# An mLSTM layer with a top-1 mixture of experts on one core: first token lists gathered a step sooner without their gates, gates fetched by a second gathering, and an opening with other fills, copies and an earlier embedding

## The chip, the core and the metric

One core of one Trainium2 chip runs the kernel. Its engines work side by side and wait for each other by semaphores: TensorE (PE in the rows; PEld is its loading of weights), VectorE (DVE), ScalarE (ACT), GpSimd (POOL) and SyncE (SP), which here only issues transfers. The metric is device time in microseconds (us) of one execution; lower is better. In the rows of the profile POOL's and SP's queues are marked POOLq and SPq.

## The reference

The first half is a recurrent layer with gates (4 batches, 8 heads, 768 time steps, 40 dimensions per head), the second a mixture of 8 experts in which each of the 3072 tokens goes to the one expert with the largest logit.

```python
for t in range(S):                                   # q, k, v: (4, 8, 768, 40)
    m_new = np.maximum(f_gate[:, :, t] + m, i_gate[:, :, t])
    f_stab = np.exp(f_gate[:, :, t] + m - m_new)
    i_stab = np.exp(i_gate[:, :, t] - m_new)
    m = m_new
    C = f_stab * C + i_stab * einsum('bhd,bhe->bhde', vt, kt)
    n = f_stab * n + i_stab * kt
    y[:, :, t] = sigmoid(o_gate[:, :, t]) * (C @ qt) / np.maximum(np.abs(n . qt), 1.0)
x = y.transpose(0, 2, 1, 3).reshape(3072, 320)

xn, en = x / (norm(x) + 1e-6), emb / (norm(emb) + 1e-6)
logits = xn @ en.T / tau
expert_idx = argmax(logits, axis=1)
gate_w = softmax(logits)[arange(N), expert_idx]
for e in range(8):                                   # w1: (8, 320, 1024), w2: (8, 1024, 320)
    mask = expert_idx == e
    out[mask] = gate_w[mask, None] * (np.maximum(x[mask] @ w1[e], 0.0) @ w2[e])
```

## The kernel before

The recurrence is worked in 24 steps (NS; `for n in range(NS)`, line 1213), each of them 128 time steps of one batch with its 8 heads; tile n is block n // 4 of batch n % 4. In each step TensorE forms the scores of the next tile (`stage_scores`), the products of k with u·v that update the state (`stage_add`), the output y (`stage_y`) from the weighed scores and the state, the transposes of an earlier x (`stage_xt`) and the logits of a still earlier one (`stage_logits`). VectorE weighs the scores (`stage_weigh`), scales the state (`stage_next`), divides y (`stage_den`, `stage_x`); GpSimd forms u·v (`stage_uv`) and multiplies x by its output gate (`stage_gate`; VectorE in the last two steps); ScalarE copies the state for y (`stage_mid`, `stage_keep`), applies the sigmoids and sums squares. `stage_store` writes x to `x_d` in DRAM, whose rows have 336 columns: 320 of x and 16 that all hold the token's gate weight.

The order is written out by hand: every engine has one queue and works it in the order of the program text. The opening (lines 1012 to 1086) loads the first tiles, keeps TensorE at work with products that nobody reads (`fill`, FILLS), and computes the first block's gate factors. The later blocks' factors come from a chain: `gates_ends`, `gates_chain` (a scan over the blocks, between two groups of three copies across partitions by `same`, all on VectorE, ahead of the loop), `gates_floor` and `gates_exp` in steps 0 and 1, `gates_turn` in step 2. ScalarE's exponential and sigmoid need different tables; small instructions on `maxc` (lines 1076, 1236, 1291) load them ahead of use. The expert embeddings are scaled in steps 2 to 4 (`embeddings`, EMB_AT) and are first used by the logits of step 4.

Tokens are routed in three groups of tiles, 0 to 5, 6 to 12, 13 to 23 (GROUPS). The table ROUTE (line 954) says in which step which part runs: the products of a step are issued at once, its VectorE work goes into a queue `vq`, of which `tick(9)` takes nine instructions a step and the next `route` the rest. After the second group `early_ids` writes `ids_a`: for each of the two fullest experts the first 256 of its tokens among tiles 0 to 12. `gates_early` has three parts for the gate weights of these 13 tiles: [0] root, [1] share, both on VectorE, and [2], the DMA that puts the weights into columns 320 to 335 of `x_d` (line 472). Step 20 issues [2], step 21 the gathers (`gather_a`, four indirect DMAs by GpSimd's queue into `xs_a`, 128 rows each). Step 23 transposes `xs_a` on TensorE (`x_tile`, line 352), and after the loop the hidden products of these two experts (`first_hidden`, `mm1`, line 374) fill TensorE while the third group is routed. Their outputs are scaled by the gates in `xs_a` (`first_out`, `mm2_out`) much later, under the hidden products of the two experts' second halves, whose rows come by `gather(slots_b)` (line 1445). The weights of an expert are loaded raw by SP and split into a high and a low part (`piece`, lines 195 to 198), those of the first expert in the steps of W1_AT.

The places that the change touches in the loop:

```python
            if n == NS - 4:
                gates_early[2]()
            ...
                    stage_gate(k, G if n < NS - 2 else V)
            ...
            if n == NS - 3:
                for i in range(NE * HT):
                    gather_a(*divmod(i, HT))
```

## Time and profile before

| what | value |
| --- | --- |
| median of 3 runs | 322.53 us (321.46 to 325.38) |
| the profiled execution | 318.54 us |
| its span, first to last instruction | 316.8 us |
| mean granted clock of TensorE | 0.985 of full speed |
| busy: TensorE, its weight loads, VectorE, ScalarE, GpSimd | 93%, 89%, 68%, 53%, 53% |
| DMA traffic | 63.32 MB, mean 200 GB/s |

The rows further down are of that one profiled execution, with times from the start of its span. A busy TensorE is not one at its peak: its matmuls are pipelined and their ends modelled. A wait is put down to what came last. The share of an engine over the whole span is a mean over stages: the opening, the steps of the recurrence, the end of the routing, and the experts.

### The profile page before, as it was taken

What the parts mean: (1) busy time and instruction counts of PE and PEld (TensorE: products, weight loads), DVE (VectorE), ACT (ScalarE), POOL (GpSimd) and SP (SyncE); (2) the same over time, 40 slices, a digit from 0 to 9 for tenths busy, and PEclk for the clock granted to TensorE, in tenths of its full rate; (3) what the DMA queues carried; (4) which work ended last, traced back from release to release, by engine and by line L of the source; (5) the groups of instructions that cost most, each with busy time, mean ns of one, the idle gap of its engine ahead of it and who ended that gap; (6) DMA issues with size and microseconds to landing.
All of it is one profiled execution on the core that took longest, in us unless ns stands there. A gap on an engine that the chain in (4) does not pass through costs nothing. (4 is left out here: it accounts for less than half of the span.)

```text
span 316.8 us, 9586 instructions
## 1 busy us (share of the span) xinstructions
PE 296.0 (93%) x3637; PEld 281.9 (89%) x3637; DVE 216.4 (68%) x608; ACT 167.1 (53%) x429; POOL 168.7 (53%) x205
## 2 busy tenths in 40 slices
PE   7798999999994999999999899999999999999992
PEld 3788989999883899899999689999999999999991
DVE  5776798979983479856744986575576685787520
ACT  7575866776872485343343564355457267255310
POOL 7877867778786288140765622620830822633112
PEclk9999999999999699999999999999999999999998
DMA  6898887989899641130588949959639949646001
GB/s 203 303 297 302 254 266 223 311 258 272 282 252 270 215 138 41 13 88 2 180 260 228 310 161 212 326 156 344 152 117 266 259 137 320 165 119 206 23 24 38
DMA packets 47962, 63.32 MB, mean 200 GB/s; under 512 B 21018, under 2 KB 37862, under 8 KB 47906
## 3 DMA queue, kind: packets, MB, share of 16 engines
q1 hardware_dynamic: 45234, 54.16, 57.3%
q0 software_dynamic: 2560, 8.35, 8.6%
q8 instruction: 31, 0.51, 0.7%
q14 instruction: 25, 0.20, 0.2%
q10 hardware_dynamic: 112, 0.10, 0.1%
HBM read 47.51 MB, written 11.93 MB: 188 GB/s over the span
## 5 line engine op out<-in xcount | busy, mean ns | idle before, releaser
L425 POOL DMA_INDIRECT out<-ob,ids x20 | 22.4, 1121 | 77.0 <-DVE ob L422 66.9
L376 ACT ACTIVATE hh<-ph 128x448 fp32r<-128x448 f32 (+2 forms) x48 | 23.4, 490 | 39.9 <-PE ph L374 29.1
L406 PE MATMUL po<-w2h,hl 128*128 128x320 f32 x128 | 39.6, 309 | 0.0
L406 PE MATMUL po<-w2h,hh 128*128 128x320 f32 x128 | 39.6, 309 | 0.0
L406 PE MATMUL po<-w2l,hh 128*128 128x320 f32 x128 | 39.5, 309 | 0.0
L556 POOL TENSOR_TENSOR uv<-kv_s,u_t 64x328 f32<-64x328 f32 x47 | 35.1, 747 | 6.7 <-PE c L610 4.0
L374 PE MATMUL ph<-xh,w1h 128*128 128x448 f32 (+2 forms) x96 | 32.1, 337 | 2.0 <-DVE hh L381 2.0
L379 DVE SCALAR_TENSOR_TENSOR hl<-ph,hh 128x384 fp32r<-128x384 f32 (+1 forms) x48 | 24.4, 508 | 11.5 <-ACT hh L376 11.4
L374 PE MATMUL ph<-xh,w1l 128*128 128x448 f32 (+2 forms) x96 | 32.0, 336 | 0.0
L195 ACT CAST w1h<-raw 128x512 fp32r<-128x512 f32 x48 | 29.0, 612 | 5.3 <-POOL halves L1468 2.9
L571 PE MATMUL s<-kq_s 128*64 128x64 f32 x768 | 28.3, 226 | 2.6 <-DVE w_s L580 2.1
L571 PEld LDWEIGHTS s<-kq_s 128*64 128x64 f32 x768 | 26.1, 141 | 3.9 <-DVE w_s L580 2.8
L198 DVE TENSOR_TENSOR w2l<-raw,w2h 128x320 fp32r<-128x320 f32 x58 | 27.6, 523 | 1.2 <-issue 0.4
L195 ACT CAST w2h<-raw 128x320 fp32r<-128x320 f32 x62 | 24.9, 458 | 6.3 <-DMA raw<-in_w 6.1
L422 DVE TENSOR_SCALAR ob<-po,gt 128x320 f32<-128x320 f32 x16 | 8.8, 550 | 27.4 <-PE po L406 27.4
L198 DVE TENSOR_TENSOR w1l<-raw,w1h 128x512 fp32r<-128x512 f32 x36 | 25.5, 717 | 1.5 <-ACT w1h L195 1.4
L297 POOL DMA_INDIRECT xs<-x_d,ids x20 | 22.1, 1103 | 6.2 <-issue 5.8
L374 PE MATMUL ph<-xl,w1h 128*128 128x448 f32 (+2 forms) x96 | 24.5, 336 | 0.0
L653 PE MATMUL y<-uv,w_s 128*64 128x82 f32 x384 | 24.2, 245 | 0.0
L406 PEld LDWEIGHTS po<-w2h,hh 128*128 128x128 f32 x128 | 24.0, 188 | 0.0
L406 PEld LDWEIGHTS po<-w2l,hh 128*128 128x128 f32 x128 | 24.0, 188 | 0.0
L406 PEld LDWEIGHTS po<-w2h,hl 128*128 128x128 f32 x128 | 24.0, 188 | 0.0
(315 smaller groups left out, 891.7 us busy)
## 6 DMA issues: line engine op xcount, KB each, us to landing
raw<-in_w SPq DMA_DIRECT2D x32, 320.0 KB
kv_s<-in_kv SPq DMA_DIRECT2D x24, 324.0 KB
kq_s<-in_kq SPq DMA_DIRECT2D x48, 160.0 KB
raw<-in_w SPq DMA_DIRECT2D x14, 512.0 KB
raw<-in_w SPq DMA_DIRECT2D x18, 256.0 KB
sig<-in_og SPq DMA_DIRECT2D x24, 160.0 KB
x_d<-x SPq DMA_DIRECT2D x24, 160.0 KB
x_d<-halves SPq DMA_DIRECT2D x4, 576.0 KB
```

The lines of the kernel that those rows point to most:

```text
L195: A.copy(h, src)
L198: (eng or V).tensor_tensor(lo, src, h.bitcast(F32), ALU.subtract)
L297: G.indirect_dma_start(out=xs[0 : c.shape[0], a], out_offset=None, in_=x_d[0:rows], in_offset=bass.IndirectOffsetOnAxis(ap=c, axis=0), bou ...
L374: T.matmul(ph, lt, rh, start=i == 0, stop=i == len(ops) - 1)
L376: A.activation(hh, ph, AF.Relu)
L379: V.scalar_tensor_tensor(hl[:, 0:m], ph[:, 0:m], 0.0, hh[:, 0:m].bitcast(F32), ALU.max, ALU.subtract)
L406: T.matmul(po[0 : ts_.stop - ts_.start, 0:DM], lt[f][:, ts_], rh[:, f], start=k == 0, stop=k == len(ops) - 1)
L422: V.tensor_scalar(ob, po[0:r, 0:DM], gate, None, ALU.mult)
L425: store = G.indirect_dma_start(out=out, out_offset=bass.IndirectOffsetOnAxis(ap=slots, axis=0), in_=ob, in_offset=None, bounds_check=NT - ...
L556: eng.tensor_tensor(uv[n % NB][rows, :, :, r], list(rows_of(n))[1][rows], u_t[rows, j, b].unsqueeze(3).broadcast_to([L, 2, NP, D1]), ALU.mult,
L571: T.matmul(s[r * L : r * L + L, c, p], k_of(n, odd)[:, a, cs], q_of(n)[:, a, cs], start=True, stop=True,)
L653: T.matmul(yh[c][:, g, :, odd], w_s[n % NB][:, c, 2 * g + odd], uv[n % NB][:, c, 2 * g + odd], start=g + odd == 0, stop=n < B and c == 0, ...
```

## The change

The fills become 11, 1 and 1, and the second and third place, which called none before, call them: behind the first gate products and behind the clearing of the sums. The copies across partitions of the gate chain go to ScalarE; the gathering copies stand behind `stage_mid` of step 0, the scan and the copies back behind the weighing of the second scores. `gates_floor` computes what `gates_exp` needs first, with a tile `low` of its own. The embeddings' last part stands before `stage_next` of step 4, and that step's logits behind `stage_add`. The x tiles are two named tiles of 336 columns whose last 16 are cleared once; the first 13 stores write all 336. The list `ids_a` is computed in step 19, root and share of the early gates in steps 20 and 21, their store behind the last x store. The gathers are issued in step 20 and once more behind `gather(slots_b)`. VectorE takes the gating from step 20 on, and u·v of the last tile, in step 21. One weight piece moves from step 19 to 18.

```diff
@@ -48,7 +48,7 @@
-W1_AT = (11, 13, 15, 17, 19, 21)
+W1_AT = (11, 13, 15, 17, 18, 21)
 W_AT = (9, 10, 12, 14, 16, 18, 19, 20, 21, 22, 22, 23)
@@ -58,7 +58,7 @@
 ROOTS = {6: (0, 4), 10: (4, 8), 15: (8, 13), 18: (13, 16), 22: (16, 20)}
-FILLS = (9, 3, 3)
+FILLS = (11, 1, 1)
 NK = 2
@@ -521,7 +521,8 @@
-        st, sigs, xs_, grp = {}, {}, {}, {}
+        st, sigs, grp = {}, {}, {}
+        xs_ = [tp.tile([P, B, XW], F32, name=f"x_{i}", bufs=1) for i in range(2)]
@@ -686,12 +687,9 @@
         def x_of(n):
-            return xs_[n // B][:, n % B].rearrange("p (h d) -> p h d", h=H)
+            return xs_[n // B % 2][:, n % B, 0:DM].rearrange("p (h d) -> p h d", h=H)
         def stage_x(n):
-            j, b = divmod(n, B)
-            if b == 0:
-                xs_[j] = tp.tile([P, B, DM], F32, name=f"x_{j}", tag="x", bufs=2)
             den = st[n]["den"].rearrange("p a r -> p (a r)")
@@ -701,17 +699,18 @@
             j, b = divmod(n, B)
-            SY.dma_start(xrows(j)[:, b, 0:DM], xs_[j][:, b])
+            w = XW if n < GROUPS[1][1] else DM
+            SY.dma_start(xrows(j)[:, b, 0:w], xs_[j % 2][:, b, 0:w])
...
             junk = tp.tile([P, DM], F32, name=f"junk_{n}", tag="junk", bufs=1)
-            A.activation(junk, xs_[j][:, b], AF.Square, accum_out=ss_all[:, j, b : b + 1])
+            A.activation(junk, xs_[j % 2][:, b, 0:DM], AF.Square, accum_out=ss_all[:, j, b : b + 1])
...
             j, b = divmod(n, B)
-            x = xs_[j][:, b]
+            x = xs_[j % 2][:, b]
             px = pX.tile([P, 512], F32, name=f"px_{n}", tag="px")
@@ -962,11 +961,12 @@
             15: ([], [(route_a, 1)]),
-            16: ([lambda: route_rank(1)], [(route_b, 1), (route_sum, 1), (gates_early[0],)]),
+            16: ([lambda: route_rank(1)], [(route_b, 1), (route_sum, 1)]),
             17: ([], [(route_os, 1)]),
             18: ([early_count], [(route_c, 1), (early_base,)]),
-            19: ([lambda: route_ids(1)], [(gates_early[1],), (route_d, 1)]),
-            20: ([], [(early_ids,)]),
+            19: ([lambda: route_ids(1)], [(route_d, 1), (early_ids,)]),
+            20: ([], [(gates_early[0],)]),
+            21: ([], [(gates_early[1],)]),
         }
@@ -1071,11 +1071,13 @@
                 )
+        fill(FILLS[1])
         V.tensor_copy(u_t[:, 0].rearrange("p b c a -> p c b a"), pg[:, 0:NH].rearrange("p (c b a) -> p c b a", c=2, b=B))
...
         clear_sums()
+        fill(FILLS[2])
         stage_scores(0)
@@ -1088,39 +1090,37 @@
         mm = ap1.tile([NH, NW + 1], F32, name="mm")
-        mj, aj, na, cl, gam = (ap1.tile([NG, NK], F32, name=nm) for nm in ("mj", "aj", "na", "cl", "gam"))
+        mj, aj, na, cl, gam, low = (ap1.tile([NG, NK], F32, name=nm) for nm in ("mj", "aj", "na", "cl", "gam", "low"))
         flag = ap1.tile([NG, NK], BF16, name="flag")
...
-        def same(dst, src):
-
-            V.tensor_tensor(dst, src, src, ALU.max)
-
         def gates_ends():
-            same(fp[:, :, 0], gs[:, :, P - 1])
+            V.memset(mm[:, 0:1], -1e30)
+            V.tensor_tensor(fp[:, :, 0], gs[:, :, P - 1], gs[:, :, P - 1], ALU.max)
             V.tensor_tensor(fp[:, :, 1], gp[:, :, P - 1], gs[:, :, P - 1], ALU.add)
+        def gates_gather():
+            for jj in range(NJ):
+                A.copy(fpj[:, :, :, jj], fp[jj * NH : (jj + 1) * NH].rearrange("p k w -> p w k"))
+
         def gates_chain():
-            for jj in range(NJ):
-                same(fpj[:, :, :, jj], fp[jj * NH : (jj + 1) * NH].rearrange("p k w -> p w k"))
-            V.memset(mm[:, 0:1], -1e30)
             f, p = (fpj[:, w].rearrange("p k j -> p (k j)") for w in range(2))
...
             for jj in range(NJ):
-                same(mj[jj * NH : (jj + 1) * NH], mm[:, jj : jj + NJ * (NK - 1) + 1 : NJ])
+                A.copy(mj[jj * NH : (jj + 1) * NH], mm[:, jj : jj + NJ * (NK - 1) + 1 : NJ])
...
             V.tensor_tensor(gam, mj, aj, ALU.subtract)
+            V.tensor_scalar(low, gam, -RANGE, None, ALU.max)
+            for k in range(NK):
+                V.scalar_tensor_tensor(
+                    gp[:, k], gp[:, k], na[:, k : k + 1], low[:, k : k + 1].broadcast_to([NG, P]), ALU.add, ALU.max
+                )
             V.tensor_tensor(cl, mj, gi[:, :, 0], ALU.max)
...
             V.tensor_scalar(flag, cl, -RANGE, None, ALU.is_lt)
-            V.tensor_scalar(cl, gam, -RANGE, None, ALU.max)
-            for k in range(NK):
-                V.scalar_tensor_tensor(
-                    gp[:, k], gp[:, k], na[:, k : k + 1], cl[:, k : k + 1].broadcast_to([NG, P]), ALU.add, ALU.max
-                )
@@ -1209,7 +1209,6 @@
         gates_ends()
-        gates_chain()
         for n in range(NS):
@@ -1229,6 +1228,8 @@
             stage_mid(n)
+            if n == 0:
+                gates_gather()
             for k in of(n - 1, 1, NEXT_AT):
@@ -1238,28 +1239,32 @@
                 stage_scores(n + 1)
-            if n + 2 < NS and n not in (1, 2):
+            if n + 2 < NS - 1 and n not in (1, 2):
                 stage_uv(n + 2)
             if n == 0:
-                for t in (ent, *c_st):
+                for t in (*(x[:, :, DM:] for x in xs_), ent, *c_st):
                     G.memset(t, 0.0)
-            if n == NS - 4:
-                gates_early[2]()
             if n:
...
                 for k in of(n, 1):
-                    stage_gate(k, G if n < NS - 2 else V)
+                    stage_gate(k, G if n < NS - 4 else V)
             if n == 1:
                 stage_uv(n + 2)
-            if n == NS - 3:
+            if n == NS - 4:
                 for i in range(NE * HT):
...
                 stage_weigh(n + 1)
+            if n == 0:
+                gates_chain()
+            if n == EMB_AT[2]:
+                embeddings(2)
             for k in of(n, 1, NEXT_AT):
                 stage_next(k)
+            if n == NS - 3:
+                stage_uv(n + 2, (V, V))
             if n != EMB_AT[2]:
@@ -1272,10 +1277,6 @@
                 stage_uv(n + 2)
-            if n == EMB_AT[2]:
-                embeddings(2)
-                for k in of(n, 3, (EMB_AT[2],)):
-                    stage_logits(k)
             if last:
@@ -1285,6 +1286,9 @@
                 stage_add(n, 1)
+            if n == EMB_AT[2]:
+                for k in of(n, 3, (EMB_AT[2],)):
+                    stage_logits(k)
             if n != 1:
@@ -1370,6 +1374,7 @@
         stage_store(n)
+        gates_early[2]()
         work(1, 2)
@@ -1443,6 +1448,8 @@
     xs = gather(slots_b)
+    for i in range(NE * HT):
+        gather_a(*divmod(i, HT))
     halves = lp.tile([P, NTT, 2, 3 * P], U16, name="halves", bufs=1)
```

## Rows read from the trace of the kernel before

**Rows 1.** The page: busy us, share of the span and instructions of each engine.

```profile
PE 296.0 (93%) x3637; PEld 281.9 (89%) x3637; DVE 216.4 (68%) x608; ACT 167.1 (53%) x429; POOL 168.7 (53%) x205
```

**Rows 2.** Waits of PE, whole span: who for whom, us in total, times, longest.

```profile
PE pa L352 <- DMA xs_a<-x_d,ids_a: 5.2, 1, 5.2
...
PE s L571 <- DVE w_s L580: 2.1, 3, 1.4
...
PE pm L730 <- DVE ent L1201: 1.1, 1, 1.1
```

**Rows 3.** Stretches: busy us (x instructions) of each engine, granted clock, DMA share, GB/s.

```profile
88.00:98.30 10.30, 9.84 (x255) 9.01 (x251) 7.77 (x27) 7.03 (x23) 7.19 (x9) 1.00 0.92 237
98.30:103.40 5.10, 0.00 (x0) 0.00 (x1) 1.02 (x3) 0.31 (x2) 4.17 (x5) 0.90 0.98 306
103.40:109.20 5.80, 5.77 (x47) 5.29 (x48) 2.46 (x8) 2.67 (x8) 1.31 (x3) 0.50 0.79 256
109.20:130.00 20.80, 20.48 (x200) 19.70 (x200) 17.71 (x43) 12.57 (x36) 14.20 (x13) 1.00 0.25 72
139.50:150.00 10.50, 10.24 (x79) 9.98 (x78) 4.70 (x17) 2.93 (x7) 0.00 (x0) 1.00 0.06 18
```

**Rows 4.** Timeline at the list and its gathers: start, us, engine, line, operation.

```profile
90.77 0.16 DVE L937 TENSOR_TENSOR pad_a<-thrp,cnt_a 128x4 f32<-128x4 f32 x1
...
91.17 0.72 DVE L947 TENSOR_SCALAR ids_a<-pad_a 128x4 uint32<-128x4 f32 x1
...
91.96 0.40 SPq L472 DMA_DIRECT2D x_d<-sw  x1
...
97.11 1.31 POOL L297 DMA_INDIRECT xs_a<-x_d,ids_a  x1 [2.80 <-DMA x_d<-sw]
```

**Rows 5.** The tile xs_a: its gathers (ns min/median/max), and issue to landing.

```profile
L297 POOL DMA_INDIRECT xs_a<-x_d,ids_a x4: 994/1000/1306, 97.1 to 101.3; - x4
DMA to landing us min/median/max: 5.4/6.0/6.2
```

**Rows 6.** Timeline, DVE: prices of root, share, gating and a u·v half.

```profile
6.50 0.49 DVE L556 TENSOR_TENSOR uv<-kv_s,u_t 64x328 f32<-64x328 f32 x1
...
77.95 0.45 DVE L451 TENSOR_TENSOR lg_all<-lg_all,rs 128x104 f32<-128x104 f32 x1
...
85.78 0.79 DVE L458 RECIPROCAL sn<-sn 128x104 f32<-128x104 f32 x1
...
88.53 0.37 DVE L468 COPY sw<-se 128x208 f32<-128x208 f32 x1
...
95.68 0.49 DVE L700 TENSOR_TENSOR x<-x,sig 128x320 f32<-128x320 f32 x1
...
122.54 1.03 DVE L451 TENSOR_TENSOR lg_all<-lg_all,rs 128x88 f32<-128x88 f32 x1
```

**Rows 7.** Timeline of the opening.

```profile
1.10 4.02 PE L996 MATMUL warm<-ones 128*128 128x512 bf16 x9 [1.10 <-DVE ones L510]
...
7.43 1.98 PE L571 MATMUL s<-kq_s 128*64 128x64 f32 x32
...
10.27 1.15 PE L571 MATMUL s<-kq_s 128*64 128x64 f32 x32 [0.32 <-DVE w_s L580]
...
11.16 1.28 ACT L1291 ACT_TABLE_LOAD   x1
...
11.57 1.01 DVE L1097 TENSOR_TENSOR fpj<-fp 32x4 f32<-32x4 f32 x3
...
13.77 0.69 DVE L580 TENSOR_TENSOR w_s<-s,late 128x512 f32<-128x512 f32 x1
...
15.50 0.46 PE L653 MATMUL y<-uv,w_s 128*64 128x82 f32 x8
```

**Rows 8.** Timeline, POOL behind the second lists' gathers.

```profile
150.08 1.02 POOL L425 DMA_INDIRECT out<-ob_a,ids_a  x1 [10.65 <-DVE ob_a L424]
```

**Rows 9.** Timeline, PE at step 4.

```profile
28.09 0.87 PE L730 MATMUL pm<-ent,xt 128*64 128x8 f32 x24 [1.12 <-DVE ent L1201]
```

## The prediction

> **What bounds the kernel now.** I read the busy shares first: TensorE (PE) is busy 93% of the span and no other engine comes near [rows 1], so what can be won is time in which PE waits or runs slowly. PE's waits come next: one of 5.2 us for the first gathered lists, 2.1 us in three for the weighed scores, 1.1 us for the scaled embeddings [rows 2]. The table by stretches shows what the long wait costs beyond itself [rows 3]: from 98.3 to 103.4 PE does nothing, and from 103.4 to 109.2 its granted clock is 0.50, the lower of its two levels (1.2 instead of 2.4 GHz), while PE is busy all the time. Half of those 5.8 us is lost, 2.9. So the place costs 5.1 + 2.9 = 8.0 us. From 109.2 to 130 PE is busy 20.48 of 20.8 us: what PE gains before it moves the end.
>
> Why are the lists late? `ids_a` is computed from 90.77 to 91.17 + 0.72 = 91.9. SyncE issues the store of the gates at 91.96, and GpSimd (POOL) holds the first gather until 97.11, the last 2.8 us of it for that store alone [rows 4]. The four gathers start from 97.1 to 101.3, 1.4 apart, and each takes 5.4 to 6.2 us from issue to landing [rows 5]. The first lands at 97.1 + 6.2 = 103.3, where PE starts again.
>
> **Part 1, lists and gathers.** The list moves from step 20 of the state loop to 19, the gathers from 21 to 20, the gates' store behind the last x store. On VectorE (DVE) the gates' root moves from 16 to 20 and their share from 19 to 21. In before the share runs from 85.78 to 88.53 + 0.37 = 88.9, ahead of the addition that the list needs [rows 6]. Without it that addition starts near 85.9, and the list, 1.1 us as in before, is there at 87.2. POOL comes later: in before it was free for the gathers at 97.11 − 2.80 = 94.3, in step 21. From the second weighing at 13.77 [rows 7] to the end of the last step's logits at 98.3 are 23 steps, 3.7 us each, so one step earlier is 90.6; one gating fewer on POOL brings it forward, the weight piece that moves from step 19 to 18 does not delay it further than that. Between 90 and 91, then: the first lands at 96.0 to 97.2, the second at 97.4 to 98.6. PE asks for them at 98.3 and about half a us later. The wait goes, with 1 to 2 us in hand for the first, and with it the fall of the clock: 8.0 gained.
>
> What is late next? DVE. Into steps 20 to 22 come two gatings at 0.49, two u·v halves at 0.49, the share at 3.1 us (an estimate of 2.2 if nothing slows its long instructions), and the root, whose large instruction took 0.45 in one place and 1.03 in another [rows 6]; with its two small ones I estimate 0.8 to 2.0. The list's 1.1 leaves. Sum: 0.98 + 0.98 + (2.2 to 3.1) + (0.8 to 2.0) − 1.1 = 3.9 to 6.0. DVE was busy 7.77 of the 10.3 us from 88.0 to 98.3, and 0.9 of that was the share's tail, which is in the sum already [rows 3]. So 3.0 to 5.1 us come into 2.5 us of slack: 0.5 to 2.6 shows at PE, and 5.1 if the order in DVE's queue lets none of the slack be used. But the next step's weighing stands ahead of root and share in the queue, so PE meets each delay a step later, by which time part is made good. I take 1.5. Part 1 gives 6.5; its ends are 8.0 − 5.1 = 2.9 and 8.0.
>
> The rest of part 1 is costed at nothing, by its cover. The x stores of 13 tiles become 5% wider (336 columns for 320); two small clearings stand on POOL behind the u·v of step 2. The second gathering is four more indirect DMAs, behind the second lists' own: POOL stands idle for 10.65 us up to 150.08 [rows 8], from 139.4; 4 x 1.4 = 5.6 us fit in. The first of them lands at 139.4 + 6.2 = 145.6 or earlier (DMA is at 0.06 there [rows 3]), the last at 149.8; the first row of gates is wanted just before the store at 150.08, the others later. Without that cover each us of late gates would hold DVE's queue and, behind it, the evictions of PE's hidden products.
>
> **Part 2, the opening.** The nine filling products take 4.02 us, 0.43 each, which for 512 columns is 1.2 GHz. The first scores (32 products) take 1.98, the second scores 1.15 [rows 7]. So the clock rises between 9.4 and 10.3. Behind the nine fills PE has short pauses. Eleven fills reach to about 1.10 + 11 x 0.43 = 5.8 and hold the first gate product by some 0.25; the two single ones fill pauses. If unbroken work lifts the clock before the first scores, these take 1.98 − 1.15 = 0.8 less and their additions about 0.3 less; less the 0.25, 0.9 gained. If not, the fills cost 0.25 to 0.6.
> By the Trainium skill (TensorE: Matmul & The Clock Gate, "What's actually happening") the half rate is the default, activity releases it, and the monitor runs freely, not from the kernel's start; by it the sum holds the 0.9 in some executions and not in others.
>
> The chain of gate maxima moves too. In before DVE copies across partitions, three in 1.01 us and three back, ahead of the weighing of the second scores: ready at 10.27 + 1.15 = 11.4, weighed at 13.77. Now ScalarE (ACT) makes these six copies, as an estimate 0.15 each, and the weighing comes first, near 11.6. But ACT has its own chain: a sigmoid, a table load of 1.28 [rows 7], then the copy of the mid state that the second y reads. That load ran at 11.16, under DVE's chain; now it stands behind the gates: 11.5 + 0.5 for the gather, 0.2 for the scan, 0.5 for the copies back, 0.5 for the sigmoid, 1.3 + 0.2 for the load, 0.6 for the mid state, 15.3. The second y began at 15.50 [rows 7]. So here almost nothing is gained, and some 0.4 at the next scores, whose weighing has fewer floors ahead of it. Opening in all: 1.3 at best, −0.6 at worst; taken 0.8, nearer the good end because in before too the clock rose once PE worked without pauses.
>
> **Part 3, the embeddings.** PE waits 1.12 us at step 4 for `ent` [rows 9], which DVE copies behind two scalings of the state. Now it copies first, and the logits stand behind y and the additions. The wait goes whole; taken 1.0 (0.5 if y then meets the later scalings). The stretches from step 5 on show no such wait to swallow it [rows 2].
>
> **Sum.** 6.5 + 0.8 + 1.0 = 8.3, taken as 8. The profiled execution took 318.54 us, 316.8 of span and 1.74 around it: 310.5. It lies 4.0 below the median of the runs shown, 322.53; no row says what those lost, so I take the same 8 from the median: 314.5.
>
> **Rivals.** (a) VectorE takes the gathers' place: no slack is used, steps 20 to 23 grow by 5.1, part 1 leaves 2.9; with 1.8 elsewhere 4.7, so 317.8. For it: DVE is busy 0.75 of that stretch before anything is added [rows 3]. Against it: the queue order above. (b) The gathers still land late: their 6 us belong to a stretch with DMA at 0.92 to 0.98 [rows 3]; at 9 us, or with POOL held a step longer, a wait of 3 us stays and the clock falls with it. Then some 1.5 of part 1 and 1.8 elsewhere remain: 319.2. Against it: the four landings lie within 0.8 us of each other [rows 5].
> The Trainium skill (SBUF — State Buffer, "SBUF: two separate sides") says that DVE copies in a two-port mode keep GpSimd from writing descriptors, so that gathers beside DVE work starve. Here the longest generation is 1.31 us against a median of 1.00 [rows 5], which bounds it; by the rule a landing moves by the length of such copies, 0.37 for the share's last.
> (c) Slower: VectorE's 5.1 comes as one gap of PE in steps 21 to 23 and the clock falls there. 9 us of work at half rate lose 4.5; 5.1 + 4.5 − 8.0 = 1.6, and with fills that cost 0.6 and embeddings at 0.5 the sum is 1.7 slower: 324.2. It decides if PE stands still there in one piece, as it did from 98.3 until its clock fell. (d) Everything hits: 8.0 + 1.3 + 1.1 = 10.4, so 312.1.
>
> **How the numbers follow.** Forecast 0.62, with its own range 312.5 to 317 (6.5 ± 1.2 of part 1 and the two ends of the opening), (a) 0.15, (b) 0.10, (c) 0.06, (d) 0.07. The range 309.5 to 319.5 holds the forecast, (d) with 2.6 to spare for what the runs' 4 us hide, (a) and most of (b); it leaves out (c) and tails, under 2 in 10. Two per cent, about what a measurement of this kernel can tell from no change, is 6.45 us, so faster needs 316.1 or less: (d) and nine tenths of the forecast, 0.62. Slower means 329: the far end of (c) and what I did not think of, 0.06. The rest is 0.32.
>
> **What would show it.** Right: no wait of PE for `xs_a`; granted clock 1.00 from step 20 through the tail; the first gather issued near 90 us; first scores near 1.2 us; no wait for `ent`. Wrong: PE waiting for `w_s` or x in steps 21 to 23 by over 2 us; a clock of 0.50 in the 90s; DVE waiting for `xs_a` at the first outputs with PE held behind; hidden products of the first lists waiting for weights that still land at the old time.

## The result, and the profile after

The changed kernel takes 325.54 us (median of 20 runs, 322.85 to 329.30) where the kernel before takes 322.36 (20 runs, 319.42 to 328.01). The ratio is 1.0124, with a 95% interval of 1.0097 to 1.0152: slower by 1.2%. Ratios here leave out executions that took over 1.5% longer than the quickest of the same kernel, so they need not be the quotient of the two medians. The forecast was 314.5, the range 309.5 to 319.5. The direction was wrong, and rival (c), the slower one, is not what happened either.

The waits of TensorE in the changed kernel (columns: engine, instruction, what it waited for, total us, times, longest):

```profile
PE pt L338 <- DVE xl_p L341: 3.1, 1, 3.1
PE ph L374 <- issue: 2.5, 1, 2.5
PE s L572 <- issue: 1.9, 2, 1.0
PE s L572 <- DMA kq_s<-in_kq: 1.5, 2, 1.0
PE y L665 <- ACT c_mid L627: 1.2, 1, 1.2
PE c L611 <- DVE c L634: 1.2, 1, 1.2
```

The waits for `xs_a` and for `ent` of [rows 2] are both gone, as predicted. In their place stand waits of which [rows 2] shows next to nothing. "issue" means that PE waited for nothing that the profile shows. In the steps of the recurrence up to 88 us its own next instructions were not there (last section); the 2.5 us, ahead of 162.53, are another thing: PE follows VectorE's `hl_b`, and that ScalarE's `hh_b`, held until 161.64 as told below. The stretches that answer to [rows 3], with 40 to 60, the stretch behind PE's longest wait and one near the end added (columns: us, then busy us and instructions of each engine, granted clock, DMA share, GB/s):

```profile
40.00:60.00 20.00, 18.06 (x459) 16.48 (x454) 15.44 (x55) 12.15 (x39) 12.71 (x16) 1.00 0.90 288
98.30:103.40 5.10, 4.74 (x80) 4.43 (x78) 4.76 (x13) 2.46 (x8) 2.28 (x3) 0.67 0.41 150
103.40:109.20 5.80, 5.75 (x108) 5.23 (x105) 5.20 (x16) 4.52 (x15) 0.10 (x1) 1.00 0.60 176
140.00:150.00 10.00, 6.93 (x41) 6.65 (x40) 2.32 (x7) 1.65 (x3) 2.93 (x3) 0.84 0.22 63
146.80:150.10 3.30, 3.30 (x14) 3.30 (x13) 1.03 (x5) 0.58 (x1) 0.00 (x0) 0.50 0.00 0
160.00:200.00 40.00, 37.03 (x227) 35.81 (x227) 26.50 (x64) 18.24 (x39) 20.38 (x21) 0.96 0.80 227
```

From 103.4 to 109.2 PE now does 108 instructions at the full clock, where it did 47 at half. But from 140 to 150 it does 41 where there were 76 from 140 to 150 before, and it is idle for 3.1 us. Behind the gaps the granted clock falls: it is 0.50 from 99.0 to 102.3 and again from 146.8 to 150.1, a sign of being wrong that the prediction named ("a clock of 0.50 in the 90s"). The timelines of PE, ScalarE and POOL show what stands there (start, duration, instruction, and in brackets the idle time before it with what ended it):

```profile
140.64 0.60 PE L338 MATMUL pt<-ident,xs 128*128 128x128 f32 x4
...
138.18 0.38 ACT L376 ACTIVATE hh_a<-ph 128x256 fp32r<-128x256 f32 x1 [0.43 <-remote]
144.86 1.07 ACT L340 CAST xh_p<-pt 128x512 fp32r<-128x512 f32 x2 [6.29 <-remote]
...
138.63 0.99 POOL L297 DMA_INDIRECT xs_a<-x_d,ids_a  x1 [0.30 <-issue]
142.54 1.00 POOL L297 DMA_INDIRECT xs_a<-x_d,ids_a  x1 [0.30 <-issue]
```

The cast of the later slots' rows waits only for PE's transposes. The records of the first four of them end by 141.24. It begins at 144.86, 1.3 us after POOL has issued the last gather of the second gathering. "remote" means that the page finds no instruction that ended just before the release. The trace has the times at which semaphores rise, and they tell more: the cast waits for a semaphore that only TensorE's instructions raise, and the rises for these four products stand at 144.73 to 144.84, 3.6 us or more behind the ends of their records. So it is TensorE's signal that comes late here, not ScalarE that is slow. VectorE's rest `xl_p` and the third turning wait behind it. The same thing stands in steps 21 and 22, where the first gathering now runs (POOL issues it from 92.95 to 98.3): two engines stand still until about the time that POOL is done, and TensorE's signals of 94.59 and 95.37 rise at 98.12 and 98.95.

```profile
98.15 0.69 DVE L581 TENSOR_TENSOR w_s<-s,late 128x512 f32<-128x512 f32 x1 [3.31 <-remote]
98.98 0.48 ACT L719 COPY xt<-px 128x384 f32<-128x384 f32 x1 [3.14 <-remote]
```

The table follows the lead through the kernel: starts of some weighings `w_s`, of the first hidden products, and the span, each from the trace named. The first two columns are the traces of [rows 1] and of the result; the next two are from one chip ("chip 0"), the last from another ("chip 6"). Both are experiments below.

| us | before | changed | before, chip 0 | changed, chip 0 | changed, chip 6 |
| --- | --- | --- | --- | --- | --- |
| weighing of step 6 | 32.27 | 30.68 | 32.78 | 29.97 | 30.38 |
| step 10 | 48.13 | 45.93 | 48.09 | 45.45 | 45.81 |
| step 12 | 54.85 | 55.05 | 55.16 | 55.23 | 54.10 |
| step 18 | 77.12 | 78.09 | 77.43 | 78.54 | 76.12 |
| step 21 | 89.94 | 90.35 | 90.25 | 91.74 | 88.49 |
| first hidden product of the first lists | 107.90 | 107.56 | 105.91 | 108.23 | 101.52 |
| first hidden product of the later slots | 145.94 | 150.14 | 143.95 | 150.60 | 139.00 |
| span | 316.8 | 323.3 | 317.5 | 323.7 | 310.4 |

The lead of 2.2 us at step 10 is lost by step 12; the sooner lists leave 0.3 us at the first hidden product; at the later slots' product the changed kernel is 4.2 behind, at the end 6.5. The medians differ by less than these spans, 3.2 us: both traces of before are of executions below its median (318.5 and 319.3 us, where its runs beside these kernels lay between 317.6 and 328.0). Nor is the lead always lost by step 12: `e1` below, the same program up to there, weighs steps 12 and 18 at 53.02 and 75.07.

### The profile page after: what moved, and what is told of

The parts are those of the page before. It is cut to its first block, busy times and chain, and to the rows that moved or that the text cites. A ratio compares the mean times of both kernels' runs of the same rounds, so it can differ in the third digit from the quotient of the medians.

```text
span 323.3 us, 9613 instructions
## 1 busy us (share of the span) xinstructions
PE 300.6 (93%) x3641; PEld 284.5 (88%) x3641; DVE 218.3 (68%) x606; ACT 168.1 (52%) x435; POOL 171.1 (53%) x207
## 4 chain that ended last, share of the span: by engine, by line
PE 73%; DVE 12%; another core or an unknown queue 5%; DMA 3%; ACT 2%; issue 2%; POOL 0%; POOLq 0%; SPq 0%; DVEq 0%
PE ph L374 28%; PE po L406 17%; PE s L572 5%; PE po_b L406 4%; PE y L654 4%; DMA kq_s<-in_kq 3%; PE c L611 3%; PE po L391 3%; PE y L665 3%; DVE op L895 2%; PE pm L729 2%; PE px L715 1%; PE po_a L406 1%; DVE w_s L581 1%
## 5 line engine op out<-in xcount | busy, mean ns | idle before, releaser
L557 POOL TENSOR_TENSOR uv<-kv_s,u_t 64x328 f32<-64x328 f32 x45 | 33.8, 750 | 7.1 <-PE c L611 2.9
L572 PE MATMUL s<-kq_s 128*64 128x64 f32 x768 | 29.2, 227 | 3.4 <-issue 1.9
L572 PEld LDWEIGHTS s<-kq_s 128*64 128x64 f32 x768 | 26.9, 141 | 4.4 <-issue 3.2
L198 DVE TENSOR_TENSOR w1l<-raw,w1h 128x512 fp32r<-128x512 f32 x36 | 27.3, 769 | 0.0
L198 DVE TENSOR_TENSOR w2l<-raw,w2h 128x320 fp32r<-128x320 f32 x58 | 26.5, 503 | 0.6
L581 DVE TENSOR_TENSOR w_s<-s,late 128x512 f32<-128x512 f32 x24 | 16.5, 687 | 12.4 <-PE s L572 9.0
```

Of the source, the lines that this page charges most:

```text
L198: (eng or V).tensor_tensor(lo, src, h.bitcast(F32), ALU.subtract)
L557: eng.tensor_tensor(uv[n % NB][rows, :, :, r], list(rows_of(n))[1][rows], u_t[rows, j, b].unsqueeze(3).broadcast_to([L, 2, NP, D1]), ALU.mult,
L572: T.matmul(s[r * L : r * L + L, c, p], k_of(n, odd)[:, a, cs], q_of(n)[:, a, cs], start=True, stop=True,)
L581: V.tensor_tensor(w_s[n % NB].rearrange("p c a t -> p (c a) t"), st[n]["s"].rearrange("p c a t -> p (c a) t"), late.unsqueeze(1).broadcast ...
```

## Experiments

Ratios are to the kernel before, run beside each kernel on the same chip.

**One part taken away or alone (chip 11; before 319.03).** `e1_no_second` leaves the second gathering out, and with it the gates of these lists:

```diff
     xs = gather(slots_b)
-    for i in range(NE * HT):
-        gather_a(*divmod(i, HT))
```

> The changed kernel without its second gathering: the four lists keep the rows' gates at zero, so their part of the output is left out; everything else stays. Theory S: ScalarE's cast of the rows xh_p, which in the changed kernel begins 3.6 us after its transposes (144.86, with the extra gathers on POOL from 138.63 to 143.54), is held by the second gathering. Then the cast follows the transposes within 0.2 us as before, and the time falls by 4 to 5 us below the changed kernel's 325.5, to about 321. Theory R: the stall has another cause (instructions that arrive late, whatever the gathers do) and the loss sits in the recurrence, where the scores of step 21 came 2 us later. Then the time stays at 325 within 1 us, and a stall of some us stands in the same place or near it.

Measured: 313.77 us, 0.9914 (0.9872 to 0.9955). `e2_second_early` keeps the second gathering and moves it:

```diff
         work(3)
         tick(9)
+        for i in range(NE * HT):
+            gather_a(*divmod(i, HT))
         route_rank(g)
```

> The changed kernel with the second gathering moved ahead: POOL issues it right after the rows' last turning in the drain (about 110 us) instead of behind the gathering of the later slots (138.6). Theory S (the gathers hold ScalarE's cast because they are under way when it is due): about 321, no stall at the cast; POOL's splits of weights behind them come 5.2 us later and have 6.6 us of POOL's idle time before the later slots' gathering to hide in. Theory R: 325 within 1 us. If the gathers hold whatever ScalarE does at the time: a stall of 3 to 6 us on ScalarE at 113 to 120 us in place of the other, and 325 again.

Measured: 312.22 us, 0.9853 (0.9782 to 0.9925). `e3_opening` is the kernel before with FILLS = (11, 1, 1), the two new fills, the copies on ScalarE and the chain behind the weighing:

> The kernel before with the opening's part alone (more filling products in other places, the gates' copies on ScalarE, the chain behind the weighing). Prediction on record: 0.4 to 0.8 us gained. Rival: the second step's y waited 1.20 us for the copy c_mid of ScalarE in the changed kernel, and the scores of the second step for their input (1.05 and 0.41 us), so the opening gives nothing: within 0.5 us of the kernel before, 322.4.

Measured: 318.07 us, 0.9997 (0.9936 to 1.0059). The clock was up at the first scores (1.15 us for the 32 products, against 1.98 in [rows 7]), but the second scores then waited 0.83 us for `kq_s`. No gain can be seen. With the old fills the first scores take 1.98 us in two traces of four (the one of [rows 7] and e17) and 1.15 in the other two (e4, e6), so the faster clock is not always a gain of the new fills. `e4_lists` is the kernel before with the lists' part alone:

> The kernel before with the lists' part alone: the first lists gathered sooner without gates, the gates in a second gathering, VectorE's and POOL's work moved; the opening and the embeddings stay as before. Prediction on record for this part: 6.5 us gained, 316. Theory S: the gain of the sooner lists (about 1 to 2 us by the changed kernel's trace, where the first hidden product stands 0.9 us sooner) less 5 us at the cast: about 326. Theory R, where the loss is in the recurrence and comes from the opening or the embeddings: about 321.

Measured: 315.44 us, 0.9948 (0.9901 to 0.9994), near neither theory's number. e1 and e2 lie 7 and 9 us under the 321 of theory S: none of these four traces shows a "remote" stall on ScalarE or VectorE, so on this chip there was nothing for either theory to explain. What they show is the wait that the prediction expected next, VectorE's queue. In e1, VectorE (lines between them left out):

```profile
92.83 0.68 DVE L581 TENSOR_TENSOR w_s<-s,late 128x512 f32<-128x512 f32 x1
93.43 1.01 DVE L557 TENSOR_TENSOR uv<-kv_s,u_t 64x328 f32<-64x328 f32 x2
94.48 0.80 DVE L458 RECIPROCAL sn<-sn 128x104 f32<-128x104 f32 x1
...
97.48 0.37 DVE L468 COPY sw<-se 128x208 f32<-128x208 f32 x1
97.77 0.16 DVE L683 SCALAR_TENSOR_TENSOR den<-y,e_t 128x8 f32<-128x8 f32 x1
...
99.40 0.69 DVE L581 TENSOR_TENSOR w_s<-s,late 128x512 f32<-128x512 f32 x1
```

and PE:

```profile
100.14 0.55 PE L352 MATMUL pa<-ident,xs_a 128*128 128x128 f32 x3 [1.81 <-DVE w_s L581]
```

The u·v halves and the share, from 93.43 to 97.85, stand ahead of the denominators and so of the last weighing; PE's turning of the gathered rows needs the scores' PSUM tile, which that weighing frees. This wait stands in seven traces of this study, 1.8 to 1.9 us long.

**The changed kernel, the kernel before and two variants (chip 0; before 322.23).** `e5_after_again` and `e6_before_again` are the two kernels unchanged, `e2b_second_early` is e2 again, and `e7_share_22` is e2 with one edit more:

```diff
-            21: ([], [(gates_early[1],)]),
+            22: ([], [(gates_early[1],)]),
```

> The changed kernel once more, unchanged, beside its variants on one chip. The moved second gathering stood at 0.985 of the kernel before, the kernel without it at 0.991. If the second gathering in its old place costs 4 to 5 us whenever it runs: 1.005 to 1.012 of the kernel before, with ScalarE's cast xh_p 3 us or more behind its transposes. If the stalls of 3 to 6 us on ScalarE and VectorE (98, 145 and 162 us) belong to that one execution and not to the program: 0.985 to 0.995 of the kernel before, and no such stall in this trace.

> The kernel before, unchanged, to see its trace a second time. The prediction took its 5.15 us wait for the first lists' rows as the cost of every execution. If it is: PE waits 4.5 to 5.5 us before the rows' turning. If the wait is only what is left when PE runs ahead (the opening alone showed 0.77 us there, with the last product of the recurrence 2.1 us later): the wait is 1 to 5 us, and the later the recurrence's end, the shorter. Ratio 1.000 within 0.6%.

> The changed kernel with the second gathering ahead in the drain, once more, beside the changed kernel on the same chip. If the place of the second gathering decides: 0.980 to 0.990 of the kernel before and 1.5 to 2.5% under the changed kernel. If it does not: within 0.5% of the changed kernel.

> The same with one edit more: the shares of the gates (VectorE, 3.2 us: six operations from the reciprocal to the copy sw) run at step 22 in place of 21. In the runs so far they stand ahead of the step's denominators, and so ahead of the last weighing w_s, on VectorE, and PE waits 1.8 us for w_s before it turns the first rows. If VectorE's queue is what holds the end of the recurrence: that wait is gone and the time 1 to 2 us under the kernel with the second gathering moved alone. If it only moves the wait (the turned rows' rests xl_a stand behind the shares then): within 0.5 us of it.

Measured: e5 324.50 us, 1.0112 (1.0060 to 1.0164); e6 322.71, 1.0000; e2b 321.86, 1.0009 (0.9957 to 1.0062); e7 322.28, 0.9999 (0.9954 to 1.0044). The stall at the cast is in e5 again:

```profile
145.37 1.07 ACT L340 CAST xh_p<-pt 128x512 fp32r<-128x512 f32 x2 [6.22 <-remote]
```

Moving the second gathering into the drain takes it away and is worth 1.0% (1.0112 to 1.0009), some 3 us. In e2b the cast follows its transposes:

```profile
142.33 0.59 ACT L340 CAST xh_p<-pt 128x512 fp32r<-128x512 f32 x1 [2.88 <-PE pt L338]
```

POOL issues the second gathering there from 122.0 to 127.0, and no engine has unexplained idle time; between 122.9 and 126.4 no signal of TensorE is due. The kernel before shows no 5 us wait here, but VectorE, ScalarE and PE held while POOL issues the first gathering (95.9 to 101.1). From e6, VectorE, ScalarE and two of PE's five small gaps:

```profile
101.88 0.17 DVE L682 SCALAR_TENSOR_TENSOR den<-y,e_t 128x8 f32<-128x8 f32 x1 [3.93 <-remote]
...
101.98 0.60 ACT L626 COPY c_mid<-c 40x164 f32<-40x164 f32 x2 [3.27 <-remote]
...
100.31 0.34 PE L730 MATMUL pm<-ent_p,xt 128*64 128x8 f32 x5 [0.39 <-issue]
101.03 0.34 PE L730 MATMUL pm<-ent_p,xt 128*64 128x8 f32 x5 [0.39 <-issue]
```

e7 settles nothing: here the held `w_s` (3.28 us at 99.84) covers the queue that it was to shorten.

**What of a gather holds the engines (chip 13; before 319.54).** `e8_twice` runs the loop of the second gathering twice (`range(2 * NE * HT)`); `e9_narrow` reads as many rows, 64 bytes each, from a view of `x_d` with 16 columns:

```diff
-        gather_a(*divmod(i, HT))
+            out=xs_a[:, e, a, 0:16],
+            in_=x_d.rearrange("r (g o) -> (r g) o", o=16)[0 : GROUPS[1][1] * P],
```

> The changed kernel with its second gathering done twice: eight gathers of 128 rows behind those of the later slots, where it has four (the output stays the same). In its two traces ScalarE's cast xh_p began 1.3 us after POOL had issued the last gather (143.5 and 144.9), though its transposes had ended 3 us earlier. Theory H (ScalarE gets its next instruction only when POOL has issued its gathers): four gathers at 1.30 us each more, the cast comes 5.2 us later still, and the time is 4 to 5 us above the changed kernel, about 1.025 of the kernel before. Theory F (one piece of ScalarE's program arrives late, once): the cast stays 3.5 us behind its transposes, the time within 1 us of the changed kernel.

> The changed kernel with a second gathering of as many rows but 64 bytes of each in place of 1344 (the rows' gates stay zero, so the four lists' part of the output is left out). If the bytes of the gathered rows hold ScalarE's cast: it follows its transposes within 1 us, and the time is 3 to 4 us below the changed kernel, about 1.000 of the kernel before. If it is POOL's issuing of descriptors, whatever they move: the same stall of 3 us or more, within 1 us of the changed kernel.

Measured: e8 329.11 us, 1.0281 (1.0128 to 1.0433); e9 325.18, 1.0202 (1.0111 to 1.0293). The cast, in e8 and in e9:

```profile
147.53 0.58 ACT L340 CAST xh_p<-pt 128x512 fp32r<-128x512 f32 x1 [9.10 <-remote]
```

```profile
143.46 1.07 ACT L340 CAST xh_p<-pt 128x512 fp32r<-128x512 f32 x2 [6.30 <-remote]
...
141.15 1.00 POOL L1453 DMA_INDIRECT xs_a<-x_d,ids_a  x1 [0.30 <-issue]
```

With a twentieth of the bytes the stall is the same, 1.3 us past the last issue (142.15): it is not the rows' bytes. With eight gathers it grows by 2.8 us, where theory H gave 5.2 and theory F nothing. The cast comes before the eighth is issued (147.60), so "only when POOL has done" is too simple: the late signals rise one by one from 146.01 to 147.51. A late piece of program (theory F) is not the cause: in the changed kernel no packet of the instruction queues moves between 134.6 and 152.3. The changed kernel itself was not run on this chip; these stalls are compared with its traces from others.

`e10_late_weights` moves weight loads out of steps 9 to 12:

```diff
-W1_AT = (11, 13, 15, 17, 18, 21)
-W_AT = (9, 10, 12, 14, 16, 18, 19, 20, 21, 22, 22, 23)
+W1_AT = (14, 15, 16, 17, 18, 21)
+W_AT = (12, 13, 14, 15, 16, 18, 19, 20, 21, 22, 22, 23)
```

> The changed kernel with the first expert's first four loads three, three, two and one step later (steps 12, 13, 14, 15 in place of 9, 10, 12, 14) and the pieces that use them at 14, 15, 16 in place of 11, 13, 15. In the traces the changed kernel is 2.6 us ahead at the weighing of step 10 and level with the kernel before at step 12: PE waits there three times 0.9 to 1.0 us for its own next instructions (43, 49, 55 us) and 1.4 us for kq_s, with the transfers at 0.87 to 0.89. If the weights' loads in steps 9 to 12 make these late: the lead at step 12 is 2 us or more, and PE's waits of 0.9 us between 43 and 56 are gone; the time falls only if the lead survives steps 12 to 19, into which the loads move. If the lead is lost for another cause (PE's order, VectorE's queue): level at step 12 again.

Measured: 326.48 us, 1.0243 (1.0108 to 1.0379); step 12 weighed at 54.63, as in e8 (54.63), and PE still waited 0.69 us for instructions at 54.24. Nothing shows that these loads eat the lead. `e11_open_emb` is e3 with the later embeddings:

> The kernel before with the opening's part and the later embeddings alone; lists and gathers stay as before. Prediction on record: 0.8 and 1.0 us, 1.8 together, 0.994 of the kernel before. If the inputs' transfers swallow any lead of the opening by step 12, and the first lists' rows are waited for at the end anyway: 1.000 within 0.4%.

Measured: 320.91 us, 1.0100 (1.0004 to 1.0197). Its lead over e6 (chip 0) was 2.4 us at step 12 (52.72 against 55.16) and 1.4 at step 21 (88.84 against 90.25); then the engines were held under the first gathering, VectorE for 3.29 and ScalarE for 4.15 us, and the first hidden product came at 106.44, 0.5 behind e6.

**The first gathering's place (chip 6; before 319.77).** `e14_after_mark` is the changed kernel, `e15_second_early` is e2, and two variants of e2 move the first gathering:

```diff
 e12_spread
-            if n == NS - 4:
-                for i in range(NE * HT):
-                    gather_a(*divmod(i, HT))
+            if n >= NS - 4:
+                gather_a(*divmod(n - NS + 4, HT))
 e13_gather_21
-            if n == NS - 4:
+            if n == NS - 3:
```

> The changed kernel unchanged, as the mark for the other three on the same chip: 1.008 to 1.015 of the kernel before.

> The changed kernel with the second gathering alone moved ahead into the drain. If ScalarE's held cast is the larger part of the loss: 3 to 4 us under the mark (1.000 of the kernel before, as on the last occasion). If the place of the second gathering is of no weight here: within 1 us of the mark.

> As the second gathering moved, and the first gathering's four issues, which stand in one run at step 20, spread: one each at steps 20, 21, 22 and 23. If the run of four is what holds VectorE, ScalarE and PE at steps 21 and 22 (2 to 4 us in every trace on such a chip): no stall over 1 us there, and 2 to 3 us under the second gathering moved alone (about 0.993 of the kernel before). If the rows of the last two lists then come too late: PE waits for xs_a in the drain, 2 us or more, and nothing is gained. If the stall comes at each single gather: no change.

> As the second gathering moved, and the first gathering in one run at step 21 in place of 20, where it stood in the kernel before (the lists are ready for it a step sooner than before). If the sooner gathering costs because it stands under the last steps of the recurrence: 1 to 2 us under the second gathering moved alone. If the rows then are waited for: 1 to 3 us over it, with PE waiting for xs_a. If the run's place is of no weight: within 0.5 us.

Measured: e14 313.00 us, 0.9831 (0.9767 to 0.9895); e15 314.41, 0.9834 (0.9775 to 0.9893); e12 316.27, 0.9890 (0.9825 to 0.9955); e13 315.99, 0.9834 (0.9741 to 0.9927). The mark itself missed its expectation by three per cent: on this chip the unchanged program of the result is 1.7% faster than the kernel before. The cast stands right behind its transposes, with POOL issuing the same eight gathers beside it (127.0 to 137.7):

```profile
134.95 0.59 ACT L340 CAST xh_p<-pt 128x512 fp32r<-128x512 f32 x1 [4.03 <-PE pt L338]
...
135.44 1.00 POOL L297 DMA_INDIRECT xs_a<-x_d,ids_a  x1 [0.30 <-issue]
```

Where nothing is held, the second gathering's place is of no weight (e15 against e14), nor is one step at the first (e13); spreading gives no gain.

**The spread version on one more chip (chip 4; before 322.27).** `e16_spread_again` is e12, `e17_before_third` the kernel before.

> The version with the second gathering moved into the drain and the first gathering's four issues one each at steps 20 to 23, once more. If this chip holds the engines while POOL issues a run of gathers (then the trace of the kernel before beside it shows VectorE or ScalarE idle for 2 us or more at 95 to 102): single issues show no stall over 1 us, and the ratio is 0.990 to 0.997, under the 1.001 that the run of four gave. If single gathers hold the engines too: 1.000 or more. If this chip holds nothing: 0.985 to 0.992 as on the last occasion.

> The kernel before, unchanged, for its trace on the same chip. Where the engines are held: VectorE or ScalarE idle 2 us or more while POOL issues the first gathering, and PE's wait for the rows under 1 us. Where they are not: no such idle time, and PE waits 1 to 5 us for the rows xs_a.

Measured: e16 319.98 us, 0.9978 (0.9923 to 1.0033), just above the 0.990 to 0.997 that was expected if single issues help; e17 322.41, 1.0036. This chip holds engines too: in e16 ScalarE is idle 3.50 us ahead of 156.53, under the next expert's gathers. But from 91 to 101.5, with the first gathering spread, no "remote" or "issue" stall is over 0.5 us; only the queue's wait for `w_s` is left, 1.91 us. TensorE's signals are still late there, by up to 1.3 us (that of 93.36 rises at 94.69), against 3.6 us under the run of four in the changed kernel. That the spreading is what keeps the engines free is not shown: e17, with its run of four, has no hold at that place either; its run began at 99.42, when the recurrence had nearly ended. e17 shows the third form of one place, PE waiting for the rows after all:

```profile
PE pa L352 <- DMA xs_a<-x_d,ids_a: 6.3, 2, 5.5
```

**Over all.** On chips 6 and 11 none of eight traces has a "remote" stall, and no VectorE stall over 0.5 us that the trace leaves unexplained. On the others (the result's, 0, 13 and 4) the eleven traces have them in varying number. The version with the second gathering moved stood at 0.9853, 0.9834 and 1.0009; none of its ratios shows it slower than the kernel before beyond the interval. Each chip was used on one occasion alone, so chip and occasion can't be told apart.

The semaphores' times tell the two kinds apart more sharply. All 41 "remote" stalls of over 1 us in these twenty traces end 0.02 to 0.03 us behind a rise of TensorE's semaphore, while POOL issues indirect DMAs or at most 1.4 us behind. In e14 the rise stands 0.01 us behind the end of the product's record; in the changed kernel it came 1.2 to 3.9 us behind under the two gatherings. Of some 1,160 rises that TensorE, VectorE and ScalarE make, 71 to 98 have no record in the eleven traces, at most 3 in those of chips 6 and 11, and none is missing in the trace of [rows 1]. So the trace from which the prediction read its prices has no late signals, and that of the result has.

## Why the prediction was wrong, step by step

Two steps failed: the second gathering, which was costed at nothing by its cover, and the 8.0 us of the wait for `xs_a`, read from one execution and taken as the price in every one. With the first set right by e2b, chip 0 still shows 1.0009 where 0.975 was forecast; the larger part of the miss lies in the second.

**The wait for `xs_a` goes.** Right in every trace. POOL reached the first gather at 92.95 (91.09 on chip 6) instead of "between 90 and 91", which used up the 1 to 2 us in hand.

**It is worth 8.0 us.** The price came from one execution. Other traces of the old gathering show 0.8 us (e3), 6.3 (e17), and 0.3 (e6) and none (e11) with the engines held instead. On chip 6 the first hidden product stands 6.4 us ahead of the trace before (101.52 against 107.90), of which 1.45 was there at step 21: about 4.9 for the lists after VectorE's share, where the sum had 6.5. On chip 0 it stands 2.3 us behind (108.23 in e5, 105.91 in e6). The clock's part of the price, 2.9, came back under the held signals: 0.50 from 99.0 to 102.3.

**VectorE takes 1.5 of it back.** Right in place, and nearly in size: 1.8 us in seven traces, 0.7 in e14, by the share ahead of the denominators, as written. Not foreseen was 1.2 us near step 19 ("c <- DVE c" above), where PE waited for a scaling of the state that came late in the same queue.

**The second gathering is free.** This step failed. Its cover was POOL's idle time [rows 8] and the idle DMA engines [rows 3], and both were there. But TensorE, whose signals ScalarE needs in that stretch, was never asked. On chip 0 it costs 1.0%, e5 against e2b; on chip 6 no cost shows, e14 against e15. Without it e1, on chip 11, was at 0.9914, no better than e2 with it moved (0.9853).

**The opening gives 0.8.** The clock rose before the first scores, as said, though e4 and e6 show it risen with the old fills too; but the second scores then wait for `kq_s` (1.05 and 0.41 us in two steps) and the second y 1.20 for `c_mid`. The prediction had the latter ("almost nothing is gained") and not the former. e3: 0.9997.

**The embeddings give 1.0, and no later wait swallows it.** The first half is right: the lead is 1.6 us at step 6. The second half failed: by step 12 the lead is gone, 1.9 of the 2.4 us that were lost to PE's late instructions (0.91 at 49.0, 0.96 at 54.7). Not in every execution: e1 and e11 kept theirs there. [rows 2] shows next to no such wait, perhaps because PE, later by the same 2 us, did not meet it; that is not shown.

**So the sum.** Where nothing is held it comes nearer: on chip 6 a gain of 1.7%, 5.4 us, against 8. That 313.0 lies beside the 314.5 on record is in part luck, as the kernel before took 319.77 there and not 322.53. Where signals come late the parts do not add: the lead of the opening is lost, the sooner lists seem to move the hold into two steps of the recurrence (no run takes this apart), and the second gathering puts a further hold under ScalarE's cast. On rivals: (a) did not occur, VectorE took 1.8 us and not 5.1; (b) did not occur; (c) had the right sign, and its fall of the clock in steps 21 to 23, by another mechanism.

**Open.** Why TensorE's signals come late on some chips or occasions while POOL issues gathers, and whether only the signal is late or the product itself ends later than its record says. The runs show that bytes do not matter (e9), that more gathers hold longer (e8), that a run of four costs nothing where no signal is due (e2b, 122.9 to 126.4), and that signals under single issues were late by 1.3 us at most (e16). They do not show the mechanism.

## What to carry to other kernels

A wait at the end of a serial stage is the slack between two chains and must be read from several executions before it is priced; a lead won early meets waits that the old profile did not show. Before a moved run of indirect DMAs is called free, ask not only its queue and the bandwidth but which signals the other engines need in that stretch, and put it where none is due. Where an engine is idle and the page does not say for what, look at the semaphore that it waits for: here ScalarE and VectorE stood still, and TensorE's signal was late. A change of 1 or 2% belongs on more than one chip: one program stood at 0.983 and 1.012 here.

## What was not expected of the hardware

The same program took 313.0 us on one chip and 325.5 on another, while the medians of the kernel before stayed between 319.0 and 322.7.

PE's instructions arrive late at regular places. On chip 0 the changed kernel has such waits at 43.27, 49.18 and 54.84 us, 0.90, 1.02 and 0.96 long; counted in the trace's records they lie 125 and 126 products apart, each with a load of weights. The page's queues show what brings them:

```profile
q8 instruction: 31, 0.51, 0.7%
```

These packets are 16,384 bytes each in the trace. In the twenty traces PE waits 42 times for its instructions for over 0.4 us before 88 us, and each of these waits ends 1.3 to 1.7 us after such a packet has landed. The Trainium skill (Runtime: NRT & Kernel Launch, "Instruction fetch mechanics") states blocks of 16 KiB, 256 instructions, and calls the cost of crossing one mostly hidden. The size and the spacing agree, products and loads of weights together. Most crossings show no wait here; those that do cost 0.4 to 2.2 us, with a DMA share of 0.75 to 1.00 ahead of all but one of them, and they ate part of the lead.
